# Attention and GEGLU in one kernel: the zero fill of the attention-sum tile moved down, and the first unit's negated maximum moved ahead of an activation

## The chip, the cores and the metric

The kernel runs on one core of one Trainium2 chip. Its time is the device time of one execution, in microseconds (us). Three runs of the kernel before gave 2654.64, 2657.70 and 2658.63 us; the median is 2657.7 us. A separate execution was taken by the hardware profiler; the profile and the trace tell of that one.

The engines are TensorE (PE; its weight loads are listed apart as PEld), VectorE (DVE), ScalarE (ACT), GpSimd (POOL) and SyncE (SP), whose queue issues the DMA transfers here. Each works through its own queue in order and waits on semaphores of the others.

## What is computed

Input x has 2048 tokens of 576 numbers. It is normalised, and the normalised rows go into two branches that are multiplied at the end:

```python
xn = _layernorm(x, axis=-1)
s = _A_ref(xn, A_wqkv, A_wo)                           # attention, 32 heads of 18
g = _silu((_gelu(xn @ w_gate) * (xn @ w_up)) @ w_down)  # 576 -> 4608 -> 576
return x + s * g
```

Attention is the usual softmax(q k^T / sqrt(18)) v over all tokens, for each head, followed by the matrix wo. All is in float32.

## The kernel before, in words

**Precision.** A float32 matmul is made of matmuls on rounded operands: each operand is split into a rounded part (names ending in h: wh, hh, dh) and the remainder (wl, hl, dl), and three of the four products are summed. The splits are elementwise work: `split` (L93) does both halves on GpSimd (L94 the rounded part, L95 the remainder), `split_ap` (L98) the rounded part on ScalarE (L99) and the remainder on GpSimd (L100).

**Stages.** A first stage (about the first 197 us) normalises x, transposes it, and projects it to queries, keys (stored to DRAM as qk) and values (stored as vs, from tiles vn, L279). After it, TensorE works through "sections" to the end. One section (`section`, L436) is 27 pairs of matmuls that compute 128 hidden columns of gate and up (pg, pu, L369) for a block of 512 tokens. Between these pairs the section takes in "specials", which are spread evenly over the 27 places (`spread`, L57): pieces of the attention. While a section runs, the weights of the next one are loaded (raw, L113) and split on GpSimd (wh, wl), in three parts of 384 columns; the third part is issued behind the section's matmuls. Then comes `activate` (L379): ScalarE squares pg into the tile t1 (L382), VectorE (L383, L387, L390) and ScalarE (L386, L388) make gelu(gate) x up of it in t1. There is one buffer of t1. `finish` (L470) splits t1 to hh and hl, and after every second section the down weights to dh and dl. `downs` (L464) then multiplies these in the next sections: 24 matmuls for a half of the tokens (py, L406), whose sums VectorE adds into Y (L410, L412). The buffers of py are two.

Sections are counted from 0 in this document, as in the code. Sections 0 to 8 (the loop over FIRST, L756) lead in: FIRST = (0, 0, 4, 6, 6, 6, 6, 6, 6) says how many "lead" slots each of them takes. A lead slot (`lead_pair`, L687) is two matmuls of keys and queries (pm, L653), and for each a maximum over 512 scores by VectorE (mx, L654). There are three buffers of pm. From section 9 on, 128 sections (the loop at L774; n counts these from 0, so that the fifth of them is n = 4 = NA) carry the attention in full: score matmuls (pe, L684), exponentials on ScalarE (L685), and products with the values (acc, L718). A unit of attention is four heads by 512 queries, with four sections each.

**The running order around the change.** TensorE's order is the order of the source (`manual_schedule`). The order on the other engines is made by a scheduler from the program's order and its dependences, when the kernel is built, except for instructions that are kept in program order (`keep_in_program_order`). So a line that moves far in the source can move little in an engine's queue, and the reverse.

**The zero fill.** OT (L489) is the tile of attention sums, 126 x 2560 numbers, in a pool that is opened when the first stage's memory is free. It takes over memory of that stage, among it that of the value tiles vn, so that its fill with zeros (L490, GpSimd) waits for the last stores of values. OT is first written with data by `load_o` (L493), issued in the 23rd of the 128 full sections at the earliest (L577).

**The key tiles.** KS are 14 tiles of 128 x 512 (seven pairs), in the next pool. Once, all of them are filled with ones, in turns on VectorE and on GpSimd (L605; six tiles fall to GpSimd), then keys are loaded into most of their rows by DMA (L621).

**The maximum.** When a unit's 32 slots have been seen, `max_neg` (L656) takes the negated maximum over the unit (nm, L659) and splits it (m, L661, L662), three small instructions on VectorE. `max_end` (L664) turns it round with one matmul on TensorE (L667), copies the result to mr (L669), and sends it by eight transfers into rows of the query tiles (L674). For the first unit both are called in the loop over FIRST: slot 32 is passed in section 7, `max_neg` comes after that section's activation has been issued and ahead of `downs`, `max_end` behind `downs`.

Of the kernel before, what the change touches and what calls it, by code (L numbers as in the profile page):

```python
# [31 lines left out]
NS = 2 * NT  # L32
SLOTS = 8
NA = NS // SLOTS
# [18 lines left out]
def f(ap):  # L53
    return ap.bitcast(F32)
# [13 lines left out]
def kernel(ctx: ExitStack, tc: tile.TileContext, x, wqkv, wo, w_gate, w_up, w_down, out):  # L68
    nc = tc.nc
# [36 lines left out]
    def raw_tile(shape, pool=wts):  # L106
        return pool.tile(shape, F32, name="raw", tag="raw", bufs=2)

    def load_gu(t, keep=lambda i: i):

        raw = raw_tile([P, NC, P])
        for a, w in enumerate((w_gate, w_up)):
            keep(nc.sync.dma_start(raw[HR * a:HR * a + HR], w[:, t * P:(t + 1) * P].rearrange("(k p) n -> p k n", p=HR)))  # L113
        return raw, [], []

    def split_gu(w, k):
        hi, lo = (wts.tile([P, XG, P], F32R, name=m, bufs=5) for m in ("wh", "wl"))
        split(hi, lo, w[0][:, XG * k:XG * k + XG, :])
        w[1].append(hi)
        w[2].append(lo)  # L120
# [315 lines left out]
    def section(specials=(), tag="f", raw_d=None, early=None):  # L436

        n = FF["n"]
        FF["n"] += 1
        b, r = divmod(n // G, NR)  # L440
        g = n % G
        pairs, pg, pu = gate_up(tag)
        if g == 0:
            FF["hs"] = []
        keep = tc.keep_in_program_order if n == NU * NA + len(FIRST) + 1 else lambda i: i
        nxt = load_gu((n + 1) % (NR * G), keep) if n + 1 < NF else None
        if nxt:
            for k in range(NG - 1):
                split_gu(nxt, k)
        if g == G - 1:  # L450
            raw = FF["rawd"] = raw_d() if raw_d else raw_tile([P, G, D])
            nc.sync.dma_start(raw, w_down[r * G * P:(r + 1) * G * P, :].rearrange("(g p) n -> p g n", p=P))
            if early:
                FF["wd"] = early(raw)
        for p in spread(pairs, specials):
            p()
        if nxt:
            split_gu(nxt, NG - 1)
        FF["w"] = nxt
        if n + 1 < NF and (n + 1) % (NR * G) == 0:  # L460
            FF["xd"] = load_xd(b + 1)
        FF["act"] = activate(pg, pu, n < ATT.stop)
# [24 lines left out]

    op = ctx.enter_context(tc.tile_pool(name="op", bufs=1, reuse_waits="tile"))
    OT = op.tile([KO, NK, TB], F32, name="OT")  # L489
    nc.gpsimd.memset(OT, 0.0)  # L490
    OW, OG = {}, {}

    def load_o(b, k, pool=op):  # L493
# [75 lines left out]
    def tasks(n, part):  # L569
        for t in todo.pop((n, part), []):  # L570
            t()

    S2 = [None]
    for b in range(NB):
# [11 lines left out]
        for i in range(GROUPS):  # L586
            n = first + i * (1 if last else G)
# [12 lines left out]
    with tc.tile_pool(name="att", bufs=1, reuse_waits="tile") as att:  # L600
# [55 lines left out]
        def max_neg(u, keep=lambda i: i):  # L656

            nm = att.tile([P, 4 * QD], F32, name="nm", bufs=1)
            keep(nc.vector.tensor_reduce(nm, MX[u].rearrange("p a t c -> p (a t) c"), axis=AX.X, op=ALU.max, negate=True))  # L659
            m2 = NM[u] = att.tile([P, 2, 4 * QD], F32R, name="m2", bufs=2)  # L660
            nc.vector.tensor_copy(m2[:, 0], nm)  # L661
            nc.vector.tensor_tensor(m2[:, 1], nm, f(m2)[:, 0], op=ALU.subtract)  # L662
# [24 lines left out]
        def lead_pair(s):  # L687

            for a in range(2):
                max_mm(*divmod(s, NS), a)  # L690
# [64 lines left out]
        slot, chunk = 0, 1  # L755
        for n, m in enumerate(FIRST):  # L756
            none = [lambda: None]
            section((n == 2) * 4 * none + [lambda s=s: lead_pair(s) for s in range(slot, slot + m)] + (m > 0) * none,
                    "s" if n == 1 else "f", lead_raw)
            slot += m  # L760
            while n > 0 and chunk < KB and chunk * SLOTS <= slot + SLOTS:
                load_k(chunk, tc.keep_in_program_order)
                chunk += 1
            if n == 3:
                load_q(1)
            if n >= len(FIRST) - 2:
                load_v(n - len(FIRST) + 2)
            if slot >= NS > slot - m:
                max_neg(0, tc.keep_in_program_order)
            downs()  # L770
            if 0 in NM:
                max_end(0)
            finish(cut=split_ap)
        for n in range(NU * NA):  # L774
            u, i = divmod(n, NA)
            s0 = n * SLOTS
            section([p for s in range(s0, s0 + SLOTS) for p in slot_pairs(s)])
            if n > 0:
                load_k(n - 1 + KB)
            load_v(n + 2)  # L780
            if i == 1 and u + 2 < NU:
                load_q(u + 2)
            gates()
            tasks(n, 0)
            um, im = divmod(s0 + LEAD + SLOTS, NS)
            if im == 0 and um <= NU:
                max_neg(um - 1)
            for kt in range(i * SLOTS // 2, (i + 1) * SLOTS // 2):
                values(u, kt)
            if im == 0 and um <= NU:  # L790
                max_end(um - 1)
            tasks(n, 1)
            downs()
            tasks(n, 2)
            finish()


    with tc.tile_pool(name="epi", bufs=1, reuse_waits="tile") as epi:
        S2[0] = epi.tile([P, TB // P, D], F32, name="S2")
        XX = epi.tile([P, TB // P, D], F32, name="XX")  # L800
        n = NU * NA
# [80 lines left out]
```

## Time and profile before

| | |
|---|---|
| median of three runs | 2657.7 us (2654.64 to 2658.63) |
| profiled execution | 2656.42 us, of which the span is 2654.6 us |
| TensorE's granted clock, mean | 0.998 |
| instructions | 55995 |
| first stage, on TensorE | until 196.8 us |
| section 0, 1 and 2 begin, on TensorE | 197.4, 203.6 and about 210.4 us |
| section 3 begins | 228.1 us |
| section 8 begins | 287.4 us |

How it is read: a timeline row has the start in us from the span's start, the time in us, the engine, the line of the source, the operation, the tiles it writes and reads, how many instructions are merged into the row, and in brackets how long the engine had been idle before it and who ended that. The trace's "PEclk" is the clock that TensorE was granted, 1.00 being full speed. A "pieces" row of the chain of work has start, time and what.

### The profile page before, as it was taken

Reading aid. Unit: us, or ns where it says so; the run is one execution under the profiler, and the core shown is the slowest. Engines: PE = TensorE matmul, PEld = TensorE weight load, DVE = VectorE, ACT = ScalarE, POOL = GpSimd, SP = SyncE. Lnnn points to the kernel's source line nnn. Section 1 sums busy time; section 2 is a strip of 40 time slices with the busy share of each in tenths; the row PEclk is TensorE's granted clock in tenths of the full one; section 3 lists DMA queues with packets and bytes.
Section 4 is the critical chain, followed back from the end, with each engine's and each line's share of the span. In section 5 each row is a group of like instructions: output and inputs, shape, how many; then the busy total and the mean of one; then the engine's idle time right before and its main releaser. Section 6 shows DMA issues by size and latency. Waiting matters only on the chain.

```text
span 2654.6 us, 55995 instructions
## 1 busy us (share of the span) xinstructions
PE 2639.3 (99%) x21032; PEld 2050.3 (77%) x21032; DVE 1999.4 (75%) x3440; ACT 1506.3 (57%) x2690; POOL 1392.4 (52%) x1488
## 2 busy tenths in 40 slices
PE   9999999999999999999999999999999999999999
PEld 8887777777777777777777777777777777777788
DVE  5327888888887888777888887778888877788445
ACT  3222466666666666555666665556666655566632
POOL 2126544545466555555447655555446755555564
PEclk9999999999999999999999999999999999999999
DMA  8875433334355434444346444435335444444341
GB/s 259 267 239 140 114 99 102 97 103 103 96 126 135 106 99 107 122 114 120 103 110 146 124 102 106 119 101 134 102 100 126 134 115 122 108 111 119 77 108 60
DMA packets 390874, 323.66 MB, mean 122 GB/s; under 512 B 105736, under 2 KB 305928, under 8 KB 390604
## 3 DMA queue, kind: packets, MB, share of 16 engines
q1 hardware_dynamic: 390604, 320.08, 45.3%
q8 instruction: 167, 2.74, 0.5%
q14 instruction: 103, 0.84, 0.1%
HBM read 266.58 MB, written 52.85 MB: 120 GB/s over the span
## 4 chain that ended last, share of the span: by engine, by line
PE 97%; POOL 1%; DVE 1%; DMA 0%; issue 0%; ACT 0%; SPq 0%; POOLq 0%; DVEq 0%
PE pg L369 27%; PE py L406 18%; PE acc L718 17%; PE pe L684 10%; PE pm L653 9%; PE pu L369 7%; PE po L159 7%; PE po L550 2%; PE po L212 0%; PE pt L221 0%; POOL wl L95 0%; PE pm L667 0%; DMA den<-rT 0%; DVE thl L377 0%; DMA vs<-vn 0%
## 5 line engine op out<-in xcount | busy, mean ns | idle before, releaser
L685 ACT ACTIVATE pT<-pe 128x512 f32<-128x512 f32 x2048 | 1165.2, 598 | 703.7 <-PE pm L653 533.5
L654 DVE TENSOR_REDUCE mx<-pm 128x1 f32<-128x512 f32 x2048 | 1289.1, 684 | 52.8 <-PE pm L653 32.2
L369 PE MATMUL pg<-xd,wh 64*128 64x512 f32 x2592 | 949.3, 398 | 0.5 <-issue 0.5
L369 PE MATMUL pu<-xd,wh 64*128 64x512 f32 x2592 | 948.9, 398 | 0.0
L684 PE MATMUL pe<-q,KS 56*128 56x512 f32 x2048 | 816.9, 406 | 0.0
L653 PE MATMUL pm<-KS,q 54*128 54x512 f32 x2048 | 796.5, 395 | 4.0 <-DVE mx L654 4.0
L369 PEld LDWEIGHTS pg<-xd,wh 64*128 64x128 f32 x2592 | 483.5, 187 | 66.3 <-issue 31.8
L94 POOL TENSOR_SCALAR wh<-raw 128x384 fp32r<-128x384 f32 x432 | 226.6, 525 | 557.0 <-PE pu L369 336.7
L369 PE MATMUL pg<-xd,wl 64*128 64x512 f32 x1296 | 508.1, 392 | 0.4 <-POOL wl L95 0.4
L369 PE MATMUL pu<-xd,wl 64*128 64x512 f32 x1296 | 508.0, 392 | 0.0
L369 PEld LDWEIGHTS pu<-xd,wh 64*128 64x128 f32 x2592 | 484.4, 187 | 6.2 <-DVE t L387 0.2
L718 PE MATMUL acc<-pT,VS 128*32 128x512 f32 x4096 | 466.0, 595 | 0.0
L95 POOL TENSOR_TENSOR wl<-raw,wh 128x384 fp32r<-128x384 f32 x432 | 440.5, 1021 | 34.3
L684 PEld LDWEIGHTS pe<-q,KS 56*128 56x128 f32 x2048 | 370.6, 184 | 80.9 <-ACT pT L685 20.5
L653 PEld LDWEIGHTS pm<-KS,q 54*128 54x128 f32 x2048 | 377.0, 185 | 30.1 <-DVE mx L654 6.4
L412 DVE TENSOR_TENSOR Y<-py,Y 128x288 f32<-128x288 f32 x544 | 248.4, 457 | 188.6 <-PE py L406 187.6
L406 PE MATMUL py<-dh,hh 128*128 128x288 f32 x1152 | 352.8, 306 | 1.8 <-DVE Y L410 1.6
L406 PE MATMUL py<-dl,hh 128*128 128x288 f32 x1152 | 339.6, 295 | 0.0
L406 PE MATMUL py<-dh,hl 128*128 128x288 f32 x1152 | 338.6, 294 | 0.0
L718 PEld LDWEIGHTS acc<-pT,VS 128*32 128x32 f32 x4096 | 120.3, 109 | 276.8 <-issue 265.0
L369 PEld LDWEIGHTS pg<-xd,wl 64*128 64x128 f32 x1296 | 242.5, 187 | 18.7 <-POOL wl L95 0.8
L406 PEld LDWEIGHTS py<-dh,hh 128*128 128x128 f32 x1152 | 215.8, 187 | 44.4 <-issue 37.7
(118 smaller groups left out, 2929.6 us busy)
## 6 DMA issues: line engine op xcount, KB each, us to landing
KS<-qk SPq DMA_DIRECT2D x1536, 36.0 KB
raw<-in_B_w_gate_dram SPq DMA_DIRECT2D x144, 288.0 KB
raw<-in_B_w_up_dram SPq DMA_DIRECT2D x144, 288.0 KB
raw<-in_B_w_down_dram SPq DMA_DIRECT2D x68, 576.0 KB
VS<-vs SPq DMA_DIRECT2D x128, 152.0 KB
qk<-t SPq DMA_DIRECT2D x72, 256.0 KB
q<-qk SPq DMA_DIRECT2D x384, 36.0 KB
xd<-xhs SPq DMA_DIRECT2D x24, 384.0 KB
```

The source lines that it names most:

```text
L94: first = nc.gpsimd.tensor_scalar(hi, raw, 1.0, 1.0, op0=ALU.mult, op1=ALU.mult)
L95: nc.gpsimd.tensor_tensor(lo, raw, f(hi), op=ALU.subtract)
L159: nc.tensor.matmul(o, st, m, start=(i == 0), stop=(i == len(TERMS) - 1))
L369: nc.tensor.matmul(o, w[1 + wp][k][rr, c, :], xd[xp][k][rr, c, :], start=(i == 0), stop=(i == len(terms) - 1))
L406: nc.tensor.matmul(py, a[:, tt], w[:, g, cc], start=(n == 0), stop=(n == 3 * G - 1))
L412: nc.vector.tensor_tensor(yy, py, yy, op=ALU.add)
L550: nc.tensor.matmul(po[:, 0:288], o[x][0:n, k, :], OW[w][0:n, k, :], start=(m == 0), stop=(m == len(terms) - 1))
L653: nc.tensor.matmul(pm, QS[u, r][rr, t * P:(t + 1) * P], KS[(u * NA + c) % KB][r][rr, :], start=True, stop=True)
L654: nc.vector.tensor_reduce(MX[u][:, 2 * r + a, t, c:c + 1], pm, axis=AX.X, op=ALU.max)
L684: nc.tensor.matmul(pe, KS[(u * NA + c) % KB][r][rr, t * P:(t + 1) * P], QS[u, r][rr, :], start=True, stop=True)
L685: nc.scalar.activation(PT[u, kt][:, 2 * r + a, :], pe, AF.Exp, scale=SCALE)
L718: nc.tensor.matmul(ACC[u][32 * a:32 * a + 32, :], VS[(u * NA + c) % VB][:, v:v + 32], pt[:, a, :], start=(kt == 0), stop=(kt == NT - 1), s ...
```

## The change

Two edits. First, the fill of OT with zeros is no longer issued where OT is made, but in the loop over the full sections, in the fifth of them (n = NA). Second, `max_neg` of the first unit is no longer called after section 7 has been issued. It is passed to that section as its last special, so that it is issued behind the section's last score maxima and in front of its activation.

```diff
@@ the pool of OT
     OT = op.tile([KO, NK, TB], F32, name="OT")
-    nc.gpsimd.memset(OT, 0.0)
     OW, OG = {}, {}
@@ the loop over FIRST
             none = [lambda: None]
-            section((n == 2) * 4 * none + [lambda s=s: lead_pair(s) for s in range(slot, slot + m)] + (m > 0) * none,
+            end = [lambda: max_neg(0, tc.keep_in_program_order)] if slot + m >= NS > slot else none
+            section((n == 2) * 4 * none + [lambda s=s: lead_pair(s) for s in range(slot, slot + m)] + (m > 0) * end,
                     "s" if n == 1 else "f", lead_raw)
...
-            if slot >= NS > slot - m:
-                max_neg(0, tc.keep_in_program_order)
             downs()
@@ the loop over the full sections
             gates()
+            if n == NA:
+                nc.gpsimd.memset(OT, 0.0)
             tasks(n, 0)
```

In the built program, the fill of OT stands on GpSimd seven places further down than before: behind the six fills of KS and the rounded part (wh) of one weight split, and ahead of that split's remainder (wl), all of section 0. It waits for the same transfers as before. On VectorE the three instructions of `max_neg` stand behind the twelve maxima of section 7 and ahead of L383, where they stood between that activation's last instructions and the last two additions to Y. On SP the eight transfers from mr stand ahead of one more query load than before. TensorE's and ScalarE's orders are the same as before.

## The prediction

> **What bounds the kernel now.** I read the page's busy times and its chain that ended last, then TensorE's waits, then a table by stage.
>
> ```profile
> PE 2639.3 (99%) x21032; PEld 2050.3 (77%) x21032; DVE 1999.4 (75%) x3440; ACT 1506.3 (57%) x2690; POOL 1392.4 (52%) x1488
> ...
> PE 97%; POOL 1%; DVE 1%; DMA 0%; issue 0%; ACT 0%; SPq 0%; POOLq 0%; DVEq 0%
> ```
> ```profile
> PE pm L653 <- DVE mx L654: 4.0, 1, 4.0
> ...
> PE pm L667 <- DVE m L662: 1.2, 1, 1.2
> ...
> PE pg L369 <- POOL wl L95: 0.4, 1, 0.4
> ```
> ```profile
> ...
> 210.00:214.97 4.97, 4.97 (x43) 3.73 (x39) 0.00 (x0) 0.09 (x1) 4.68 (x6) 1.00 0.53 187
> 214.97:219.00 4.03, 0.00 (x0) 0.00 (x1) 2.72 (x5) 2.25 (x5) 0.00 (x0) 0.80 0.83 190
> 219.00:224.60 5.60, 5.60 (x26) 4.18 (x26) 4.31 (x7) 1.14 (x3) 5.52 (x5) 0.54 0.92 233
> ...
> 228.10:239.70 11.60, 11.60 (x93) 9.78 (x92) 10.74 (x20) 2.35 (x4) 5.47 (x6) 1.00 0.52 143
> ...
> 286.10:299.00 12.90, 11.75 (x91) 10.04 (x92) 11.22 (x24) 3.40 (x5) 8.47 (x8) 1.00 0.40 125
> ```
>
> TensorE is the bound: busy 99%, 97% of the chain. So a change pays only where TensorE stands still, or runs at a lower clock. Three of its waits matter here: 4.0 us for a maximum (mx), 1.2 us for the negated maximum (m), 0.4 us for a weight remainder (wl). The table (after the stretch: TensorE, its weight loads, VectorE, ScalarE, GpSimd, then granted clock, DMA share, GB/s) shows a second cost of the 4.03 us wait: in the 5.6 us after it the granted clock is 0.54, against 1.00 before it and from 228 on.
>
> Behind what does that maximum stand? First GpSimd's timeline, then the rows of ScalarE, VectorE and TensorE that hang on it.
>
> ```profile
> 201.82 2.24 POOL L490 MEMSET OT<- 126x2560 f32 x1 [6.25 <-DMA KS<-qk]
> 204.00 2.87 POOL L605 MEMSET KS<- 128x512 f32 x6
> 206.84 0.52 POOL L94 TENSOR_SCALAR wh<-raw 128x384 fp32r<-128x384 f32 x1
> 207.44 1.01 POOL L95 TENSOR_TENSOR wl<-raw,wh 128x384 fp32r<-128x384 f32 x1
> 208.41 0.96 POOL L94 TENSOR_SCALAR wh<-raw 128x384 fp32r<-128x384 f32 x1
> ...
> 213.56 1.29 POOL L100 TENSOR_TENSOR hl<-t,hh 128x512 fp32r<-128x512 f32 x1
> 219.08 1.28 POOL L100 TENSOR_TENSOR hl<-t,hh 128x512 fp32r<-128x512 f32 x1 [4.24 <-ACT hh L99]
> 220.32 2.64 POOL L100 TENSOR_TENSOR dl<-pT,dh 128x1152 fp32r<-128x1152 f32 x1
> ```
> ```profile
> 209.03 0.63 ACT L99 ACTIVATE hh<-t 128x512 fp32r<-128x512 f32 x1 [1.31 <-DVE t L390]
> ...
> 214.88 0.60 ACT L382 ACTIVATE t<-pg 128x512 f32<-128x512 f32 x1 [5.22 <-POOL hl L100]
> ```
> ```profile
> 187.86 1.03 DVE L605 MEMSET KS<- 128x512 f32 x2 [0.93 <-DMA vs<-vn]
> ...
> 207.76 1.24 DVE L390 SCALAR_TENSOR_TENSOR t<-t,t 128x512 f32<-128x512 f32 x1 [1.26 <-ACT t L388]
> ...
> 217.65 0.69 DVE L390 SCALAR_TENSOR_TENSOR t<-t,t 128x512 f32<-128x512 f32 x1
> 218.26 2.48 DVE L654 TENSOR_REDUCE mx<-pm 128x1 f32<-128x512 f32 x4
> ```
> ```profile
> 214.58 0.39 PE L653 MATMUL pm<-KS,q 54*128 54x512 f32 x1
> 219.00 0.79 PE L653 MATMUL pm<-KS,q 54*128 54x512 f32 x1 [4.03 <-DVE mx L654]
> ...
> 224.58 0.40 PE L406 MATMUL py<-dh,hh 128*128 128x288 f32 x1
> 224.82 0.29 PE L406 MATMUL py<-dl,hh 128*128 128x288 f32 x1
> ```
>
> Read it backwards. TensorE has filled the three score buffers (pm) and stands until VectorE's first maximum at 218.26. VectorE is in order, and section 1's activation (L383 to L390; sections are counted from 0, as in the code) stands ahead of the maximum. That activation began at 214.88, when GpSimd's hl had let go of the one buffer t1. And hl, at 213.56, is the end of an unbroken GpSimd run that began with the zero fill of OT at 201.82, the six key-tile fills (KS) and four weight splits. The fill of OT could not start earlier: it takes over memory of the value tiles, whose last store landed only then:
>
> ```profile
> 197.31 4.21 DMA vs<-vn
> ```
>
> **The change, first edit: the fill of OT.** The fill (2.24 us) is issued in a later section of the source, but in the built program GpSimd's scheduler puts it only seven places later: behind the six KS fills and one weight split (wh), in front of that split's wl. Nothing else moves on GpSimd; TensorE's order stays, and SP's in this stretch. The fill keeps its wait for the stores, 201.52 at the end of the row above, and so still runs from 201.82 to 204.06. What changes is what is done before it: the KS fills wait for older work, the last projection's operands and stores; VectorE's own KS fills, among like memory, were through by 189 (its row at 187.86). GpSimd is free from 195.6 and now waits 6.25 us (the first row), so 2.87 us of fills and 0.52 of wh (its buffer is free some 2 us into section 0, which began after 197) fit ahead of 201.8. After it comes wl at 204.1 in place of 207.44: **3.34 us** earlier. The wait is not gone; 3.34 us of work has been moved into it.
>
> That shift travels: the later splits have their weights and buffers; hl goes from 213.56 to 210.2, still behind hh, which ends at 209.66. Then t1 is free at 211.5, the maximum ends at 215.6, and TensorE resumes at 215.66 instead of 219.00. The 0.39 us for wl disappears too, with a slow restart of some 0.3, so TensorE arrives at 214.3 in place of 214.97 and stands about 1.4 us instead of 4.03.
>
> The clock: a gap of 1.19 us stands in the stretch from 286.10, whose granted clock is 1.00. And in the 4.03 us gap the mean is 0.80: if it falls to half, it was full for the first 2.4 us. So I take a gap of 1.4 us to leave the clock at 1.00. The 5.58 us from 219.00 to 224.58 then take 5.58 x 0.54 = 3.0, and TensorE is at the down projection (py) at 218.7, 5.9 us earlier. There something is late next: the second matmul of py needs dl. Its chain (maximum's activation, hh, hl at 219.08, dl to 222.92) has moved by 3.34 only, to 219.6. So py's second matmul starts at 219.66 instead of 224.82: **5.16 us**, with some 0.75 us of new wait for dl. VectorE's maxima, 0.62 us each, two for each three pairs, cost at most some tenths before that, and these lie inside the 0.75.
>
> Does it last? The next weights are asked for at an unchanged time, since SP works in order behind key loads that do not move:
>
> ```profile
> 215.11 0.64 SPq L113 DMA_DIRECT2D raw<-in_B_w_up_dram  x1
> ...
> 305.05 0.66 SPq L113 DMA_DIRECT2D raw<-in_B_w_up_dram  x1
> ```
> ```profile
> 240.86 1.29 POOL L100 TENSOR_TENSOR hl<-t,hh 128x512 fp32r<-128x512 f32 x1 [7.21 <-PE pm L653]
> ...
> 309.69 0.51 POOL L94 TENSOR_SCALAR wh<-raw 128x384 fp32r<-128x384 f32 x1 [5.40 <-DMA raw<-in_B_w_up_dram]
> ```
>
> By the pair at 305.05 and 309.69 such a load is in after 4.6 us, here at 219.7, when GpSimd comes to it at 219.6. Section 3, now from about 223.0, has its first wl by 221.6. In that section GpSimd idles 7.21 us today, and VectorE is busy 10.74 of 11.60. I see no cover that is lost.
>
> At 207.76 VectorE's product takes 1.24 us beside GpSimd's split, against 0.69 alone at 217.65, and the split 0.96 against 0.52. I keep that 0.45 us in the chain, as the product still falls among splits; without it the gain is 0.45 more. [...]
>
> **Second edit: the negated maximum.** In section 7 the three instructions move, on VectorE alone, from behind the activation to in front of it.
>
> ```profile
> 283.09 0.69 DVE L383 SCALAR_TENSOR_TENSOR t<-t,pg 128x512 f32<-128x512 f32 x1 [0.19 <-ACT t L382]
> 283.70 0.45 DVE L412 TENSOR_TENSOR Y<-py,Y 128x288 f32<-128x288 f32 x1
> ...
> 286.33 0.21 DVE L659 TENSOR_REDUCE nm<-mx 128x16 f32<-128x64 f32 x1
> ...
> 286.82 0.16 DVE L661 CAST m<-nm 128x16 fp32r<-128x16 f32 x1
> 287.02 0.17 DVE L662 TENSOR_TENSOR m<-nm,m 128x16 fp32r<-128x16 f32 x1
> ```
> ```profile
> 284.20 0.40 PE L406 MATMUL py<-dh,hh 128*128 128x288 f32 x1
> ...
> 287.25 0.25 PE L667 MATMUL pm<-identr,m 128*32 128x128 f32 x1 [1.19 <-DVE m L662]
> ```
>
> They take 0.54 us, some 0.6 with gaps; 0.19 of that falls into an idle stretch and some of the rest into overlap, so L383 starts about 0.35 later. Behind it stands Y, which frees a py buffer for the matmul at 284.20; that one waits 0.35. VectorE's next idle, before the second Y, takes up the rest. The 1.19 us before L667 goes: **0.84 us** gained. On SP, the eight transfers of the maxima go ahead of one more query load; both are for sections from 9 on, over 10 us off. Bounds: 1.19 if nothing waits, 0.65 if all 0.54 lands on py.
>
> **Sum.** 5.16 + 0.84 = 6.0 us on the profiled execution, 2656.4 us (span 2654.6), to 2650.4. That run lies 1.3 us under the median of 2657.7; from the median it is **2651.7 us**, 0.23% less.
>
> **The rivals.** *The clock falls all the same* (chance 0.13). Two gaps, 1.4 and 0.75 us, now follow within 5 us, and only a single one of 1.19 is shown at full clock. If the clock drops as now, the stretch takes 5.58 again, py comes at 221.24, dl is there, and edit one gives 3.34: with 0.84, 4.2 us, 2653.5. [...]
>
> *The move does not work* (0.06): the KS fills wait for the same stores, since they too take over memory of that stage. Then wl stays at 207.4 and only 0.84 is left, 2656.9. Against it: VectorE's fills of the neighbours ran long before.
>
> *The gain is taken back* (0.08): TensorE, five us ahead, meets a load of weights or keys that comes by DMA at its old time. DMA is busy 0.92 in 219.00 to 224.60. It would leave 1 to 4 us, 2655. Against it the slack at 240.86.
>
> *Slower* (0.05): the lower clock does not end with the section. The stretch at 0.54 is now followed at once by dense work; if the two new gaps keep the clock at half into sections 3 and 4, each us at half costs 0.5. The 4.2 us of the first rival is used up after 8.4 us more at half; through both sections, 23 us of work, the loss is 11.6 and the time about 2665. Today's single long gap is left behind by 224.6, which speaks against it.
>
> **How the numbers follow.** My forecast has 0.68. Its own range goes from 5.0 to 6.9 (edit one 4.4 with dl's chain half a us later or slower maxima, to 5.6 without the contention; edit two 0.65 to 1.19). With the clock's rival at 4.2, and the runs shown, which spread from 2654.64 to 2658.63, I take 2649.2 to 2655.6. A difference of 0.2%, 5.3 us, is about what a measurement of this kernel can tell from none. The forecast passes that bound only by 0.7 us: faster 0.58 (most of the 0.68), same 0.37 (the rest, the clock, the lost move, most of the take-back), slower 0.05.
>
> **What would show it.** GpSimd: KS fills between 195.6 and 199, the OT fill still at 201.8, wl at 204.1. TensorE: no wait for wl, 1.4 us for the first maximum near 215, a granted clock of 1.00 after it, a new wait of 0.5 to 0.8 for dl near 219.6, no wait at L667, a short one for Y near 279. From section 3 on, everything 5.2 us earlier, from section 8 on 6.0. A wait for the maximum over 2 us, a granted clock near 0.5 behind it, or a wait for wh or wl in the following sections would make the number wrong.

## The result, and the profile after

The changed kernel takes **2651.06 us** (median of 18 runs, 2649.12 to 2652.89), the kernel before 2655.66 us in 18 runs on the same chip (2652.47 to 2658.91). The ratio is 0.9981, with a 95% interval from 0.9974 to 0.9988: by the ratio the change gains some 5.0 us, between 3.2 and 6.9 (the medians differ by 4.6). The prediction was 2651.7, 6.0 us under a median of 2657.7 from three runs; with 18 runs that median is 2 us lower.

The profiled execution of the changed kernel took 2652.89 us, the slowest of its 18; its span is 2651.1 us, against 2654.6 before. So the spans differ by 3.5 us only, and the question is where the other 2.5 us of the forecast went. In the changed kernel the lines between the two places of the fill have a number one lower (L653 is now L652).

TensorE's waits in the profile after (us in total, times, the longest):

```profile
PE py L406 <- DVE Y L410: 2.2, 2, 1.8
...
PE pm L652 <- DVE mx L653: 1.3, 1, 1.3
PE pt L221 <- DVE xx L203: 1.2, 1, 1.2
```

The wait for the maximum has gone from 4.0 to 1.3, those for m and wl are gone. But two others stand there: 1.2 us for xx, in the first stage, which the change doesn't touch, and one of 1.8 us for Y, late in the kernel. The stretches that the change does touch are best measured against section 0's first matmul, which drops the first stage. Three marks carry what follows, each the start of a row of TensorE: **s0**, section 0's first matmul (197.38 before, 198.10 after), **s3**, section 3's first score matmul, and **s8**, section 8's.

| | before | after | gain | forecast |
|---|---|---|---|---|
| s0, from the span's start | 197.38 | 198.10 | -0.72 | 0 |
| s0 to s3 (first edit) | 31.47 | 26.20 | 5.27 | 5.16 |
| s3 to s8 (second edit) | 59.37 | 58.26 | 1.11 | 0.84 |
| s8 to the end | 2366.4 | 2368.5 | -2.1 | 0 |

So in the place of the change the gain is 6.4 us, a little more than forecast; 0.7 is lost ahead of it and 2.1 behind it. First the place itself: GpSimd's timeline after, to be held against the rows of before from 201.82 on.

```profile
195.94 2.86 POOL L604 MEMSET KS<- 128x512 f32 x6
200.54 0.51 POOL L94 TENSOR_SCALAR wh<-raw 128x384 fp32r<-128x384 f32 x1 [1.73 <-PE pu L369]
202.39 2.24 POOL L783 MEMSET OT<- 126x2560 f32 x1 [1.34 <-DMA KS<-qk]
204.59 1.02 POOL L95 TENSOR_TENSOR wl<-raw,wh 128x384 fp32r<-128x384 f32 x1
...
210.75 1.29 POOL L100 TENSOR_TENSOR hl<-t,hh 128x512 fp32r<-128x512 f32 x1
216.27 1.29 POOL L100 TENSOR_TENSOR hl<-t,hh 128x512 fp32r<-128x512 f32 x1 [4.24 <-ACT hh L99]
217.53 2.65 POOL L100 TENSOR_TENSOR dl<-pT,dh 128x1152 fp32r<-128x1152 f32 x1
```

The six KS fills and a wh now run ahead of the fill of OT, in the time in which GpSimd used to stand. The fill has stayed where it was: 4.29 us after s0, against 4.44 before. The first wl comes 6.49 us after s0 in place of 10.06, so **3.57 us** earlier (forecast 3.34). Then VectorE and TensorE after:

```profile
214.84 0.69 DVE L390 SCALAR_TENSOR_TENSOR t<-t,t 128x512 f32<-128x512 f32 x1
215.45 4.86 DVE L653 TENSOR_REDUCE mx<-pm 128x1 f32<-128x512 f32 x8
```
```profile
216.19 0.49 PE L652 MATMUL pm<-KS,q 54*128 54x512 f32 x1 [1.27 <-DVE mx L653]
...
219.93 0.40 PE L406 MATMUL py<-dh,hh 128*128 128x288 f32 x1
220.24 0.40 PE L406 MATMUL py<-dl,hh 128*128 128x288 f32 x1
```

The gap is 1.27 us. From its end to py it takes 3.74 us, against 5.58 before, at a granted clock of 1.00 throughout (the table by windows below). The forecast was 3.0. VectorE works through eight maxima without a pause, 4.86 us of them, and TensorE goes at their pace. For that the wait for dl is missing: py's second matmul comes 0.31 us after the first, 0.07 more than the 0.24 of before. The sum, 0.76 (arrival at the gap) + 2.76 (gap) + 1.84 (clock and maxima) - 0.07 = 5.29, agrees with the 5.27 measured.

The second edit, VectorE and then TensorE after:

```profile
278.28 0.20 DVE L658 TENSOR_REDUCE nm<-mx 128x16 f32<-128x64 f32 x1
...
278.82 0.68 DVE L383 SCALAR_TENSOR_TENSOR t<-t,pg 128x512 f32<-128x512 f32 x1
279.42 0.91 DVE L412 TENSOR_TENSOR Y<-py,Y 128x288 f32<-128x288 f32 x2
```
```profile
279.54 0.29 PE L406 MATMUL py<-dh,hl 128*128 128x288 f32 x1
279.93 0.40 PE L406 MATMUL py<-dh,hh 128*128 128x288 f32 x1
...
281.62 0.22 PE L666 MATMUL pm<-identr,m 128*32 128x128 f32 x1
```

The negated maximum comes ahead of L383, and the matmul with it (L666 now) waits for nothing. Matmuls of py follow each other by 0.13 us; the one at 279.93 comes 0.39 after the one before, so 0.26 us are given back to Y, where 0.35 were forecast. That leaves 0.93 of the 1.19; measured are 1.11, so by estimate (1.11 less 0.93) the stop cost some 0.2 in restarting too.

Now the 2.1 us lost behind s8. In this execution they are lost near 1452 us, where a new block of tokens begins. TensorE and GpSimd after, and the same places before:

```profile
1453.62 0.40 PE L406 MATMUL py<-dh,hh 128*128 128x288 f32 x1 [1.80 <-DVE Y L410]
```
```profile
1447.72 0.62 POOL L94 TENSOR_SCALAR hh<-t 128x512 fp32r<-128x512 f32 x1
```
```profile
1458.13 0.40 PE L406 MATMUL py<-dh,hh 128*128 128x288 f32 x1 [0.80 <-DVE Y L410]
```
```profile
1452.22 0.63 POOL L94 TENSOR_SCALAR hh<-t 128x512 fp32r<-128x512 f32 x1
```

TensorE arrives 5.51 us earlier than before (1453.62 - 1.80 against 1458.13 - 0.80), but GpSimd's chain to the activation only 4.50. So 1.0 us of the gain becomes a longer wait for Y. And behind that longer wait the clock is at 0.50 for 3.41 us, as the windows of after show (busy times of TensorE, its weight loads, VectorE, ScalarE, GpSimd, then the granted clock):

```profile
212.63:216.05 3.42, 2.29 (x20) 1.86 (x17) 2.58 (x4) 1.64 (x4) 0.00 (x0) 1.00 0.39 110
216.05:219.46 3.41, 3.27 (x24) 2.14 (x25) 3.41 (x7) 1.20 (x2) 3.19 (x2) 1.00 0.85 192
1451.68:1455.09 3.41, 1.61 (x13) 1.47 (x12) 2.48 (x5) 0.52 (x2) 0.00 (x0) 1.00 0.94 223
1455.09:1458.50 3.41, 3.41 (x16) 3.41 (x16) 1.00 (x3) 0.00 (x0) 2.67 (x4) 0.50 0.85 286
1458.50:1461.92 3.42, 3.42 (x29) 2.99 (x29) 2.37 (x5) 0.90 (x2) 3.33 (x4) 1.00 0.34 105
```

In 3.41 us at a clock of 0.50, by estimate, half of them, 1.7 us of work, are lost. With the 1.0 of the wait that makes 2.7; as 2.1 are measured, the rest of the kernel would have given 0.6 back. How the windows are chosen, and what parts the 1.27 us gap, with the clock at 1.00 behind it, from the 1.80 us one, with 0.50, is told with the experiments.

### The profile page after: what moved, and what is told of

Its sections match the earlier page's. It is cut to its first block, busy times and chain, and to the rows that moved or that the text cites. A ratio compares the mean times of both kernels' runs of the same rounds, so it can differ in the third digit from the quotient of the medians.

```text
span 2651.1 us, 55993 instructions
## 1 busy us (share of the span) xinstructions
PE 2638.3 (100%) x21032; PEld 2052.5 (77%) x21032; DVE 2001.9 (76%) x3440; ACT 1506.1 (57%) x2690; POOL 1393.1 (53%) x1488
## 4 chain that ended last, share of the span: by engine, by line
PE 97%; DVE 1%; POOL 1%; issue 0%; DMA 0%; ACT 0%; SPq 0%; DVEq 0%; POOLq 0%
PE pg L369 27%; PE py L406 18%; PE acc L717 17%; PE pe L683 10%; PE pm L652 9%; PE pu L369 8%; PE po L159 7%; PE po L549 2%; PE pt L221 0%; DVE mx L653 0%; DMA xx<-in_A_x_dram 0%; PE pm L666 0%; POOL th L432 0%; DVE thl L377 0%; POOL wl L95 0%
## 5 line engine op out<-in xcount | busy, mean ns | idle before, releaser
L653 DVE TENSOR_REDUCE mx<-pm 128x1 f32<-128x512 f32 x2048 | 1289.9, 684 | 50.7 <-PE pm L652 27.2
L652 PE MATMUL pm<-KS,q 54*128 54x512 f32 x2048 | 796.2, 394 | 1.3 <-DVE mx L653 1.3
L652 PEld LDWEIGHTS pm<-KS,q 54*128 54x128 f32 x2048 | 376.5, 184 | 27.0 <-DVE mx L653 4.3
```

The lines of the kernel that those rows point to most:

```text
L652: nc.tensor.matmul(pm, QS[u, r][rr, t * P:(t + 1) * P], KS[(u * NA + c) % KB][r][rr, :], start=True, stop=True)
L653: nc.vector.tensor_reduce(MX[u][:, 2 * r + a, t, c:c + 1], pm, axis=AX.X, op=ALU.max)
```

## The experiments

**The theory** was that of the prediction: GpSimd's run of fills and splits holds the one buffer t1, t1 holds section 1's activation, that holds VectorE's first maximum, and that holds TensorE; the long gap then costs the clock. The rivals: the clock falls by itself in this stretch, whatever the gap; or the gain is VectorE's, not the buffer's; or the first edit's size isn't what the two profiles show. All times of the table are of profiled executions; "landing" is when the last of the 16 parts of the values' last store landed, from the landings in the trace, counted from s0.

| kernel | landing | gap for mx | s0 to s3 | s3 to s8 |
|---|---|---|---|---|
| before | 4.14 | 4.03 | 31.47 | 59.37 |
| before, again | 3.92 | 4.03 | 31.23 | 59.39 |
| after | 3.98 | 1.27 | 26.20 | 58.26 |
| after, again | 3.64 | 0.8 | 25.75 | 58.30 |
| first edit alone | 1.73 | 0.8 | 25.72 | 59.41 |
| first edit alone, again | 3.63 | 0.80 | 25.74 | 59.51 |
| second edit alone | 1.80 | 2.39 | 27.33 | 58.31 |
| second edit alone, again | 1.71 | 2.28 | 27.92 | 58.30 |
| 36 idle matmuls in the gap | 1.72 | none | 28.46 | 59.41 |
| two fills of OT | 4.17 | 3.68 | 30.53 | 58.29 |
| fill kept in the full sections | 3.45 | 0.44 | 25.37 | 58.29 |
| before with a second t1 | 1.73 | none | 24.75 | 59.42 |
| after with a second t1 | 1.84 | none | 24.77 | 58.28 |
| after, late fill, second t1 | 1.75 | none | 24.76 | 58.28 |

**The first edit alone.** The fill moved down, `max_neg` left where it was.

```diff
-    nc.gpsimd.memset(OT, 0.0)
...
+            if n == NA:
+                nc.gpsimd.memset(OT, 0.0)
```

> Edit one alone: the fill of OT moved, the negated maximum where it was. The yardstick is TensorE's way from the start of section 0 to section 3's first maximum matmul (before 31.48 us, changed 26.21), and from there to section 8's first maximum matmul (before 59.37, changed 58.26). My theory, that edit one moves 3.3 us of GpSimd's work into a wait and that the shorter gap spares the half clock: 26.2 and 59.4, granted clock 1.00 behind the gap, the wait of about 1.2 us before the turning matmul still there, time 0.9980 to 0.9985. Rival, that the first stretch is shorter only by the 3.3 us and the clock of this execution was luck: 27.5 to 29 and a granted clock near 0.5 again. Rival, that the gain needs both edits: over 30.

It took 2652.32 us (11 runs) against 2653.99: ratio 0.9994 [0.9985, 1.0003]. In its profile s0 to s3 is as short as in the changed kernel (25.72), s3 to s8 as long as before (59.41). So each edit works in its own stretch without the other. The time, however, hardly moves, where 0.9980 to 0.9985 were expected.

**The second edit alone.** `max_neg` moved, the fill at its old place.

```diff
     OT = op.tile([KO, NK, TB], F32, name="OT")
+    nc.gpsimd.memset(OT, 0.0)
...
-            if n == NA:
-                nc.gpsimd.memset(OT, 0.0)
```

> Edit two alone: the negated maximum moved, the fill of OT at its old place. My theory: section 0 to section 3 as before, 31.5 us with a gap near 4 us and a granted clock near 0.5 behind it; from section 3 to section 8 58.3 in place of 59.4, time 0.9996, that is about 1 us. Rival, that the three small instructions in front of the activation cost as much as they spare: 59.2 to 59.6.

2653.41 us against 2653.99: 0.9995 [0.9986, 1.0004]. s3 to s8 is 58.31: the second edit's 1.1 us are there. But s0 to s3 came out at 27.33, not near the 31.5 of before, though nothing ahead of s3 was changed.

The store, as a piece of the chain of work, and GpSimd's and TensorE's rows of this run:

```profile
197.86 1.87 DMA vs<-vn
```
```profile
200.04 2.24 POOL L490 MEMSET OT<- 126x2560 f32 x1 [3.86 <-DMA vs<-vn]
202.22 2.87 POOL L605 MEMSET KS<- 128x512 f32 x6
```
```profile
217.14 0.50 PE L653 MATMUL pm<-KS,q 54*128 54x512 f32 x1 [2.39 <-DVE mx L654]
```

The fill of OT begins 2.11 us after s0 (197.93 here), not 4.44: the store that it waits for was in after 1.87 us, where it took 4.21 in before. In before, 15 of the 16 parts of that store landed by 199.08 and the last at 201.52; here all 16 by 199.73. So the wait on which the forecast rests has **two lengths**, and the profile of before happened to show the long one.

**Filling the gap.** 36 transposes of ident into a buffer that nobody reads, ahead of the second matmul of lead slot 1: work that keeps TensorE busy while it would wait, to part the clock from the gap.

```diff
+                if s == 1 and a == 1:
+                    o = ps.tile([P, TB], F32, name="acc", tag="acc", bufs=1)
+                    for i in range(36):
+                        nc.tensor.transpose(o[:, 0:P], ident, ident)
```

> The kernel before with 36 transposes of the identity on TensorE, into the bank that the attention sums take later, in front of the matmul that waits 4.03 us. They compute nothing that is used. The scheduler puts dl one microsecond later on GpSimd with it. It parts the clock from the wait: the maximum comes as late as before. If the half clock comes from the gap: granted clock 1.00 behind it, TensorE done with section 2 about 3.7 us after it resumes in place of 5.6, then a wait for dl, and section 0 to section 3 30.4 to 30.9 us in place of 31.48. If the clock falls for another reason (the load of DMA, the kind of the work): a granted clock near 0.5 there all the same and 31.5 to 32.5.

One execution: 2655.77 us; s0 to s3 28.46, clock 1.00. That lies outside both expectations, and it decides less than was hoped. The store landed early in this run, so the gap to be filled was, by the run before this one, some 2.4 us and not 4, and the transposes took 3.88: VectorE stood 1.11 us for TensorE. That the clock stayed up with TensorE kept busy is seen once; that this is worth anything is not.

**Two fills of OT.** The changed kernel, with the fill issued twice in a row. That puts 2.24 us back into GpSimd's chain, without touching the order in front of it; in the built program the second fill stands behind the first wl.

```diff
             if n == NA:
                 nc.gpsimd.memset(OT, 0.0)
+                nc.gpsimd.memset(OT, 0.0)
```

> The changed kernel with OT filled twice, one behind the other around the first remainder, so that GpSimd's chain is 2.24 us longer. If the chain of fills, splits, hl and activation sets the first maximum: TensorE's gap grows from 1.27 to about 3.5 us. By the clock row of the kernel before (full for the first 2.4 us of its gap) the clock then falls as well, and section 0 to section 3 takes 26.2 + 2.24 + about 2 = 30.4 us. If only the wait counts and not the clock: 28.5. If the chain is not what sets the maximum: 26.2.

One execution: 2654.23 us, s0 to s3 30.53 (4.3 more than the changed kernel, for 2.24 us of GpSimd's work). TensorE, then its windows:

```profile
218.32 0.79 PE L652 MATMUL pm<-KS,q 54*128 54x512 f32 x1 [3.68 <-DVE mx L653]
```
```profile
213.83:217.24 3.41, 0.81 (x7) 0.38 (x3) 1.65 (x3) 1.71 (x3) 0.33 (x1) 1.00 0.43 128
217.24:220.65 3.41, 2.33 (x12) 1.84 (x14) 3.00 (x6) 1.68 (x2) 2.25 (x2) 0.50 1.17 230
220.65:224.07 3.42, 3.42 (x17) 2.26 (x13) 2.39 (x4) 0.16 (x1) 3.42 (x4) 0.50 0.96 265
224.07:227.48 3.41, 3.41 (x25) 3.25 (x24) 2.57 (x6) 1.56 (x3) 3.33 (x6) 1.00 0.23 66
```

The gap grows by 2.41 us, and with it the half clock is back, for 6.83 us, as expected (a gap of 3.5, 30.4 us). So the chain from GpSimd's fills to TensorE is shown by adding to it, and here the clock goes with the gap, 0.50 behind 3.68 us and 1.00 behind the changed kernel's 1.27; it does not fall by itself.

**The changed kernel, again,** to see what a second execution shows.

> The changed kernel once more, on the chip of the next three runs, so that they can be set beside it. My theory by now: how much edit one gives hangs on when the last store of values lands. In the two first profiles its last sixteenth came 2.4 us after the others (gap before 4.03 us with the half clock, way from section 0 to section 3 31.5 us before and 26.2 after); in three later profiles it came with them (27.3 us with the fill at its old place, gap 2.4 us at full clock, and 25.7 with the fill moved). So 26.2 here if the last part is late, 25.7 if not; and the time between 0.9990 (before mostly with the early landing: 1.6 + 1.1 us) and 0.9976 (mostly late: 5.3 + 1.1 us). Rival: the landing has nothing to do with it and the time is 0.9981 as in the first comparison with a way of 26.2 whatever the landing.

2651.09 us (8 runs) against 2656.79: 0.9977 [0.9967, 0.9988]. The last part of the store is late again, and s0 to s3 is 25.75, not the 26.2 that was expected for this case. This time the clock is 1.00 from s0 until the last microsecond: the half clock near 1455 belongs to the other execution, not to the kernel. But from s8 to the end 2368.0 us pass here too, 1.6 more than in before, so that the half clock is not all that is lost behind s8.

**The fill kept in the full sections.** The changed kernel, with the fill held in program order on GpSimd, so that it really runs in a later section.

```diff
-                nc.gpsimd.memset(OT, 0.0)
+                tc.keep_in_program_order(nc.gpsimd.memset(OT, 0.0))
```

> The changed kernel, with the fill of OT kept in program order, so that it stands on GpSimd in the fifth full section, some 100 instructions later. Then nothing on GpSimd waits for the stores of values before section 2. If the stores' landing is what makes edit one's worth uncertain: hl right behind hh, gap 0.7 to 0.9 us, way from section 0 to section 3 25.6 to 25.8 us whether the last part is late or not; time 0.9975 to 0.9990, the same as the changed kernel or up to 0.5 us better. Rival: the 2.24 us of fill cost TensorE something in the full section, where GpSimd is about half busy: a new wait of TensorE near 350 us and a time 1 to 2 us above the changed kernel.

2650.56 us (8 runs, 2649.53 to 2652.20) against 2656.79: 0.9977 [0.9967, 0.9988]. The tile view of OT and TensorE's row of the first maximum:

```profile
L783 POOL MEMSET OT<- x1: 2247/2247/2247, 369.9 to 369.9; 126x2560 f32 x1
```
```profile
214.40 0.50 PE L652 MATMUL pm<-KS,q 54*128 54x512 f32 x1 [0.44 <-DVE mx L653]
```

The fill now runs at 369.9, and the lead-in no longer depends on the store, which was late here too: the gap is 0.44, s0 to s3 25.37, both a little under what was expected (0.7 to 0.9, 25.6 to 25.8). TensorE has no new wait near 370. Against the changed kernel that is 0.4 to 0.8 in the profile, and nothing that the times can tell.

**Another buffer for t1, in before.** For section 1's activation alone, a buffer that is free at that time. The fill stays at its old place, ahead of everything.

```diff
-        t1 = ffn.tile([P, TB], F32, name="t1", bufs=1)
+        if FF["n"] == 2:
+            t1 = op.tile([P, NK * P], F32, name="th", tag="oh")[:, 0:TB]
+        else:
+            t1 = ffn.tile([P, TB], F32, name="t1", bufs=1)
```

> The kernel before, with section 1's activation in another tile (the memory that oh takes later), so that it need not wait until hl has read t1. Fill and maximum stand where they were. If hl's hold on t1 is the link between GpSimd's chain and the first maximum: the wait for the maximum goes altogether, granted clock 1.00, and the way from section 0 to section 3 is 25 us with an early landing of the last store and about 26 with a late one, where dl is late in its place; time 0.9980 to 0.9990. Rival: VectorE's order or the score buffers hold TensorE by themselves, and a gap over 1 us stays: 27 us or more.

2652.41 us (11 runs), ratio 0.9982 [0.9973, 0.9991]: as far as the intervals tell, as much as the whole change, with neither of its edits. ScalarE and GpSimd in this run:

```profile
210.38 0.60 ACT L385 ACTIVATE th<-pg 128x512 f32<-128x512 f32 x1 [0.59 <-PE pg L369]
```
```profile
211.55 1.29 POOL L100 TENSOR_TENSOR hl<-t,hh 128x512 fp32r<-128x512 f32 x1
```

Section 1's activation begins at 210.38, as soon as TensorE has pg, and ahead of the hl that it waited for before. GpSimd's chain is as long as ever, and the gap is gone: 24.75 us from s0 to s3. So **the one buffer t1 is the link** between GpSimd and TensorE; neither GpSimd's load as such nor VectorE's maxima are. The store landed early in this run, as in the two that follow; that the buffer does as much with a late one is argued from the chain, not shown by a trace.

**The same buffer in the changed kernel.**

> The changed kernel with the same second tile for section 1's activation. By my theory the gap of 0.8 to 1.3 us that edit one left goes too: the activation starts some 0.9 us earlier, right behind section 1's last matmul, and the way from section 0 to section 3 is 24.8 to 25.0 us, 58.3 from there to section 8; time 1 us under the changed kernel, 0.9972 to 0.9986. Rival: VectorE's eight maxima in a row hold TensorE back by themselves from then on and eat it: 25.5 us or more.

2650.25 us (9 runs), 0.9977 [0.9967, 0.9986]. s0 to s3 24.77, s3 to s8 58.28: with the buffer there, the first edit adds nothing in its stretch, and the second adds its 1.1.

**Late fill and second buffer together.** In the expectation, "section 2" and "section 1" are the sections 1 and 0 of this document's count.

```diff
-                nc.gpsimd.memset(OT, 0.0)
+                tc.keep_in_program_order(nc.gpsimd.memset(OT, 0.0))
...
+        if FF["n"] == 2:
+            t1 = op.tile([P, NK * P], F32, name="th", tag="oh")[:, 0:TB]
```

> After with both of its measures joined: the fill of OT is kept in program order on GpSimd, so that it runs in the full sections, and section 2's activation has another buffer than section 1's. If the chain from GpSimd through the one t1 to the first maximum is all that is left of the gap, neither the fill nor the buffer adds to the other: from section 0's first matmul to section 3's first score matmul 24.7 us, no gap for the first maximum, and from there to section 8's 58.3 us, as with the buffer alone; the time is that of the buffer alone, 2650.3 us. Rival: the fill still costs something in the lead-in or in the full sections: then the time differs from 2650.3 by over 1 us.

2650.17 us (11 runs) against 2655.32 (27 runs): 0.9979 [0.9971, 0.9988]. s0 to s3 24.76, no gap. As expected, neither measure adds to the other. From s0 to s8 this and the one before are 1.0 to 1.4 us shorter than the changed kernel in its two profiles; by their times no version is proved better than it.

**Each edit alone, once more, on one chip,** and before once more beside them.

> The first edit alone, unchanged from the run before, now on one chip with the second edit alone and with more rounds. Theory that the last sixteenth of the values' store sets its size: the gain is 1.6 us in executions in which that part lands with the rest and 5.3 us in those in which it lands 2.4 us later, so the mean lies between, a ratio of 0.9980 to 0.9994. Rival, that the first edit is worth the 5.2 us of the prediction in every execution: 0.9980; rival, that it is worth nothing by itself: 1.0000.

First edit: 2652.35 us (11 runs) against 2655.32: 0.9988 [0.9979, 0.9997]. Here the store landed late, and s0 to s3 is 25.74, the same as with the early store (25.72). So with the first edit the stretch hardly depends on the store; without it, it does. That the edit is worth nothing (1.0000) lies just outside this interval; the 0.9980 of the forecast lies inside this one and outside the first run's.

> The second edit alone, unchanged from the run before, on the same chip as the first alone. By the profiles 1.1 us from section 3's first score matmul to section 8's, in every execution: a ratio of 0.9996. The profile shows also whether the last sixteenth of the store is late: if it is, 31.5 us from section 0's first matmul to section 3's first score matmul and a lower clock; if not, 27.3 us and a gap of 2.4 us at full clock. Rival, that the second edit itself shortened the stretch in front of section 3 in its first run: then 27.3 with a late store too.

Second edit: 2654.27 us: 0.9996 [0.9987, 1.0005], s3 to s8 58.30. The store landed early again and the gap is 2.28 us; but s0 to s3 is 27.92, not 27.3, and the clock fell, against the expectation. TensorE's windows of this run and of the first run with the same edit:

```profile
212.87:216.28 3.41, 1.56 (x14) 1.13 (x10) 2.29 (x4) 1.63 (x4) 0.00 (x0) 1.00 0.55 146
216.28:219.69 3.41, 2.98 (x14) 2.42 (x16) 3.01 (x6) 1.49 (x2) 2.89 (x2) 0.50 1.19 226
219.69:223.11 3.42, 3.42 (x26) 2.79 (x25) 2.79 (x5) 1.15 (x3) 3.42 (x5) 1.00 0.86 254
```
```profile
213.10:216.51 3.41, 1.65 (x15) 1.22 (x11) 2.09 (x4) 1.63 (x3) 0.00 (x0) 1.00 0.45 128
216.51:219.92 3.41, 2.77 (x20) 1.73 (x22) 3.41 (x6) 1.69 (x2) 2.69 (x2) 1.00 1.19 231
```

This pair shows that the length of the gap alone does not decide the clock. The same kernel, a gap of 2.28 us in one execution and 2.39 in the other: behind the shorter one the clock was at 0.50 for a window of 3.41 us, behind the longer one at 1.00.

> The kernel before, unchanged, once more in a profile. Theory that the store's last sixteenth sets the gap: if that part lands about 4.1 us after section 0's first matmul, the wait for the first maximum is 4.0 us with the clock at about half behind it and 31.5 us to section 3; if it lands with the others, about 1.8 us after, the wait is 2.4 us at full clock and 27.3 us to section 3. Rival, that the half clock comes with this order of work whatever the store does: 31 us in both.

One execution of before: 2655.88 us. The store is late (3.92 us after s0), the gap 4.03, s0 to s3 31.23, the clock at half for 6.83 us: the profile of before again, as the theory of the late store has it.

**What holds the late part up.** The packets in the traces show what happens there. In before, 120 of the store's 128 rows (1216 bytes each) have begun by 198.66. From 199.28 to 200.20 one packet of 16 KB runs, of the queue that the profile calls "instruction" (q8), and the last eight rows, a sixteenth of the store, begin from 200.19 on. So it is in all seven executions with a late part: eight rows begin within 0.02 us of that packet's end. In the seven others all rows have ended before the packet begins (in the second edit alone 199.35 and 199.49). So in these traces the two lengths go with which comes first, the packet or the eight rows. Why the rows stand behind the packet, the traces do not show.

**The clock in the timed runs.** These have no traces, but each has its mean granted clock on record, to three places. In the traces 0.998 goes with two windows of 3.41 us at half clock (before, twice, and two fills of OT), 0.999 or 1.000 with one or none. Of the 73 timed runs of before in the three later comparisons, 25 have 0.998, and on average these took 2.3 to 2.6 us longer than the rest of their comparison. The second edit alone has 7 such runs of 22. The five kernels in which OT is filled once, and later, have none in 76 runs, and before with a second t1 has none in 11. So the long stretch at half clock is gone from the timed runs too. If a late store always leaves two such windows under the old order, as in both traces of before, it came in about a third of these runs.

**What the clock went with.** In each trace, the moments at which the granted clock changes lie apart by whole multiples of 3.413 us, from the first change near 5 us to those near 1455 and after the last matmul: in before the fall at 217.37 comes 62 of them after the first change, in after the one at 1455.09 comes 425 of them after it. So in these traces the changes lie on a grid, and where the grid lies against the kernel differs from execution to execution: a window begins 16.58 us after s0 in before (213.96), 14.53 in after (212.63). Laid on it, the windows above answer the question that gap lengths did not. With TensorE busy for 1.65 us of a window (of 3.41), or for more, the next window was at 1.00; with 1.61, 1.56, 1.09, 1.01 or 0.81, the next was at 0.50. At half, the window after one with 2.98 us of busy time, or with 3.41, was back at 1.00, and after 1.69, 1.78 and 2.33 it was not. Before, for comparison:

```profile
213.96:217.37 3.41, 1.01 (x9) 0.48 (x5) 1.20 (x2) 1.71 (x3) 0.89 (x1) 1.00 0.53 150
217.37:220.78 3.41, 1.78 (x8) 1.50 (x10) 3.26 (x6) 1.68 (x2) 1.70 (x2) 0.50 1.21 228
220.78:224.20 3.42, 3.42 (x18) 2.66 (x15) 2.58 (x4) 0.00 (x0) 3.42 (x4) 0.50 0.87 263
224.20:227.61 3.41, 3.41 (x25) 2.98 (x23) 2.18 (x5) 1.71 (x3) 3.33 (x5) 1.00 0.29 85
```

The gap of 4.03 us leaves 1.01 us of work in one window and 1.78 in the next, and the clock is at half for two windows, the second of which is wholly busy. Over the 14 profiled executions, from 8 to 2640 us, no window contradicts this. The stretches at half clock took 3.41 us (after, and the second edit alone, again) or 6.83 us (before, twice, and two fills of OT). The window ahead of the one in after, at 1451.68, was idle for 1.80 us of its 3.41, just over half.

What this says of a gap by its length is an estimate from these windows. As 1.65 us of busy time in 3.41 left the clock at 1.00, a gap below some 1.7 us would not by itself bring it down; one of 2.3 may or may not, by where it lies (2.28 did, 2.39 did not); and one of 4.03, however the windows share it, leaves one of them less than half busy, as in both executions of before (1.01 and 1.09 us).

## Why the prediction was right, and where it was not

**The end held.** 2651.06 against 2651.7, in the range, faster by 0.19% with the whole interval from 0.12 to 0.26%; the bound of 0.2% lies in the middle of it, so between "faster" and "same" the measurement itself doesn't decide. That the time is met within 0.6 us is in part luck: the median that the forecast started from was 2.0 us too high, the gain that it took off was 1.4 too large (6.0 against 4.6 between the medians), and the two errors largely cancel.

**GpSimd's shift** (forecast 3.34 us): 3.57 measured. The fill stays where it is, its wait takes in the KS fills and one wh, and a split still takes 0.96 us beside VectorE's product, as was kept in the sum. Right, and shown the other way round by the second fill, which lengthened the gap.

**The gap** (4.03 to 1.4): 1.27. **The clock** (stays at 1.00): it did. But the reason given, that the clock was full for the first 2.4 us of the old gap, was a reading of one execution: what the clock went with in the traces is TensorE's busy time in a window, at most 1.61 us ahead of a fall and at least 1.65 where it stayed at 1.00. By an estimate from these figures a gap of 1.4 us, which leaves 2.01 of 3.41 us busy, would not bring the clock down, so the forecast came out right; the window of the 1.27 us gap had 2.29 us busy. Of the first rival, two gaps of 1.4 and 0.75 us in a row, the second didn't come; and as the forecast had some 3.2 us between them, no window of 3.41 could have held both whole.

**The wait for dl** (0.5 to 0.8 us) was wrong: VectorE's eight maxima took its place, since they start late, all together. Priced as "some tenths", they cost 0.7, and dl 0.07: the end is the same, by another engine.

**The second edit** (0.84): 1.1 us in every pair of profiles. Right; Y's share was somewhat smaller than assumed.

**"Does it last?"** was answered too simply. In the profiled execution 1.0 us came back as a wait at the beginning of a block of tokens near 1452, and a window of 3.41 us at a clock of 0.50 took, by the estimate above, 1.7 us more. That is like the third rival in its outcome, but not by its mechanism: the loads there do not come at their old time (SP issues at 1435.22 a weight load that it issued at 1439.68 before); GpSimd's chain moved by 4.5 us and TensorE by 5.5.

How much of such a loss belongs to the kernel is not settled. In the changed kernel's second execution the clock didn't fall, and still 2368.0 us passed from s8 to the end, against 2366.4 and 2365.7 in the two executions of before. The six profiles that took at most 84.5 us from s0 to s8 then needed 2367.8 us on average; the seven that took 85.1 or more, the transposes aside, 2365.8. So some 2 us of what the lead-in gains seem to be taken back behind s8, which the sum put at nothing. But with the same kernel one execution differs from another here by as much: with the first edit alone, 2366.8 and 2364.6. From the matmul after the second unit's maxima to the last unit's, 2126.4 to 2130.7 us passed in the 14 executions, a scatter nearly as large as the gain. Only the times tell what lasts, 3.2 to 6.9 us.

**The step that failed is a silent one:** that the late store belongs to the kernel. The last sixteenth of the values' last store landed 3.45 to 4.17 us after s0 in seven of the 14 profiled executions, and 1.71 to 1.84 in the other seven. With the old order of the fill a late store cost 31.2 to 31.5 us from s0 to s3 (before, twice), and an early one 27.3 to 27.9 (the second edit alone, twice); with the first edit it is 25.7 to 26.2 whichever comes. So the first edit is worth about 5.4 us in the one case and 1.9 in the other. With the 1.1 of the second, that makes 4.8 us if both cases come equally often, as in the profiles, and 4.2 if the late one comes in a third, as the clocks of the timed runs suggest. Both are less than the 6.0 forecast, and both lie within the measured 3.2 to 6.9. The two lengths are shown; how often each came in the timed runs is only argued, and what is taken back behind s8 is in neither sum, so that they come near 5.0 proves little. It fits that the first edit alone measured 0.9994 and 0.9988, where 5.2 us each time would be 0.9980.

**Open** stays what decides whether the instruction packet or the store's last rows come first, and whether the place of the fill has any part in it: with the old place the store was late in two of six profiled executions, with a later one in five of eight, too few to tell.

## What to carry to other kernels

A wait for a transfer in a profile is one draw, as the store's last part was here (1.71 to 1.84 us after s0, or 3.45 to 4.17): before a gain is made of it, ask what the same wait is in another execution, and price the edit for both. Follow a wait to the buffer that hands it on: one more buffer for a single activation was worth as much here as the whole reordering. And price a gap on TensorE with the clock behind it. Here that was at 0.50 after windows of 3.41 us with at most 1.61 us busy and at 1.00 after one with 1.65, so that a microsecond more of waiting could cost more than itself: near 1452, 1.0 us cost, by estimate, 2.7.

## What was not expected of the hardware

That the changes of the clock lie on a grid of 3.413 us in each of the traces, and go with TensorE's busy time in the window before: down to 0.50 after 0.81 to 1.61 us, still at 1.00 after 1.65; from 0.50 up again after 2.98, not yet after 2.33. And a 16-way store of which one part came 1.8 to 2.5 us behind the others in half of the profiled executions, 201.52 against 199.08 in the one that the forecast was made from; its rows began when a 16 KB packet of the instruction queue ended (at 200.19 and 200.20 in that one).
